# Fused attention, gated MLP and expert attention: values loaded behind the next pair's queries and keys, MLP weights at later ranks, and zeros beside 64-row weights of the experts' tail

## The chip, the cores and the metric

The kernel is one program on one core of a Trainium2 chip. The metric is the device time in microseconds (us), of which less is better. The engines are PE (TensorE, matrix products), DVE (VectorE), ACT (ScalarE), POOL (GpSimd) and SP (SyncE, whose queue issues every load and store here). Each engine takes its instructions in the order in which they stand in its own program, and a wait holds up everything behind it on that engine.

## What is computed

Three stages follow one another: attention with a local or a strided mask, an MLP with a spatial gate, and a mixture of four attention experts of which each token takes two.

```python
B, H, S, D = 4, 8, 576, 64                        # first attention, 8 heads
scores = q @ k.T / 8                              # heads 0-3 local, heads 4-7 strided
mask_local   = (0 <= i - j < 32)
mask_strided = (i - j >= 0) and (i % 32 == j % 32)
x = softmax(where(mask, scores, -1e9)) @ v        # heads side by side: x is 4 x 576 x 512

h = relu(x @ w_in)                                # 512 -> 1024
u, vv = h[..., :512], h[..., 512:]
v_n = (vv - mean(vv)) / sqrt(var(vv) + 1e-6)
x = (u * (w_spatial @ v_n + b_spatial)) @ w_out   # 512 -> 512

logits = x @ w_gate                               # 4 experts, the best 2 weighted by softmax
for e in range(4):                                # causal attention, head dim 64
    a = softmax(causal(x @ wq[e] @ (x @ wk[e]).T / 8))
    out += gate_e * (a @ (x @ wv[e])) @ wo[e]
```

Matrix products in the second and third stage are made of three products each: an operand is split into a high part (`wh`, `xh`, `vh`) and a low part (`wl`, `xl`, `vlo`), and high by high, high by low and low by high are added up.

## The kernel before

The host of the code is a planner, the class `Plan`. Each piece of work is a generator that yields steps of the form (engine or choice of engines, planned cost, what it needs, buffers it takes), and `plan.add(rank, task)` hands it in with a rank. The planner walks through a model of the chip and always takes the step of the lowest rank that can start, so the ranks, the planned costs and the buffers that are free set the order of instructions on every engine and, where a step allows several engines, which one takes it. That order is fixed before the program runs. Buffers are counted: 75 general ones (`c`), 3 for the 512 KB blocks of the MLP's input weights (`w64`) and 8 banks of PSUM. In the first microseconds the planner fills PE's idle time with 128 by 512 products of zeros (`fill`, L217).

First attention. Heads are worked in pairs: of each batch, pairs 0 and 1 are local, 2 and 3 strided. `a1_load` (L443 on) loads a pair's queries `q` and keys `k` (288 KB each) and then its values `v` (576 KB of a local pair, 384 KB of a strided one), all in one task. `a1_scores` makes the scores on PE (L492 local, L502 strided); DVE adds the mask and takes row maxima (L515, L550: nine operations for a local pair, eleven for a strided one, each followed by a small read of the maximum); ACT takes the exponential (L521, L556); DVE sums and inverts (L529, L530); POOL or DVE scales (L532); PE transposes (L577, L579); and `a1_values` multiplies by the values (L635), after which ACT copies the high part `xh` out and DVE makes the low part `xl` (L647).

MLP weights. Of the input weights, four blocks make the half that gives vv (h = 1 in the code) and four the half that gives u (h = 0). `weight` loads a block of 512 KB (L337) and DVE takes it apart with four operations (L344, L345, L346, L349); an addition (L370) and a subtraction (L377), each on DVE or POOL, and a copy of the high part (L310 or L312) make `wh` and `wl`. The v blocks also go through PE (L357 to L359). `v_half` multiplies x by the v blocks (128 by 512 products of L289 to L291), `u_half` the u blocks by x (products of 288 columns, tiles `xh`, `xl` against `wh`, `wl`), and `spatial` the spatial weights (L789 to L791). `u_half` waits for all four u blocks.

Experts' tail. Of a batch's 576 tokens, 512 are worked in four blocks of 128 rows, and the last 64 in a fifth. `a2_tail` takes the last 64 queries of two experts, `a2_tail_turn` transposes their weights into tiles `te` (L1084), and `a2_tail_values` multiplies them by the values (L1144), ten products for a batch and a pair of experts, eight of which contract 128 rows and two 64 rows: batches are paired, and the 64 last tokens of an even batch lie in rows 0 to 63 of a shared tile, those of the odd batch in rows 64 to 127. `values` hands each batch its 64 rows of that tile.

The lines of the main program that order the work of interest:

Of the kernel before, what the change touches and what calls it, by code (L numbers as in the profile page):

```python
# [8 lines left out]
R = dt.float32r  # L9
# [144 lines left out]
def fused(tc, qk, vl, vs, win, wsb, woutT, wp, wo, out):  # L154
# [17 lines left out]
    def C(shape, dtype=F, name="c"):  # L172
        return chunk.tile(shape, dtype, name=nm(name), tag="c")
# [269 lines left out]
    def a1_load(b, hp):  # L443
        local = hp < 2
        order = [(bb, h) for bb in range(B) for h in range(4)]
        n = order.index((b, hp))
        d = 4
        prev = [("a", *order[n - d], 1)] if n >= d else []
        yield "sp", 0.46, [("a1", b)] + prev, dict(c=5 if local else 4)
        qt, kt = C([128, S], F, "q"), C([128, S], F, "k")  # L450
        nc.sync.dma_start(qt, qk[b, hp, :, 0, :])
        plan.dma(128 * S * 4)
        yield "sp", 0.46, (), {}
        nc.sync.dma_start(kt, qk[b, hp, :, 1, :])
        plan.dma(128 * S * 4)
        r = plan.ready
        st = A1[b, hp] = dict(q=qt, k=kt, nk=64 if local else 54, v=[], a={}, x=None)
        plan.set(("qk", b, hp), r - plan.end)
        if local:

            parts = [(128, 512, vl[b, hp, :, 512 * i:512 * i + 512]) for i in range(2)] + [(64, 256, vl[b, hp, :64, 1024:])]
        else:
            parts = [(128, 128 * (j1 - j0), vs[b, hp - 2, :, 128 * j0:128 * j1]) for j0, j1 in ((0, 2), (2, 6))]
        for rows, cols, src in parts:
            yield "sp", 0.46, (), {}
            t = C([rows, cols], F, "v")
            nc.sync.dma_start(t, src)
            plan.dma(rows * cols * 4)
            st["v"].append(t)
        plan.set(("v1", b, hp), plan.ready - plan.end)  # L470

    def a1_blocks(hp, g):
# [369 lines left out]
    def values(b, i):  # L842

        pair, (t0, tn) = b // 2, TB[i]
        yield ("pe", t_mm(260, 3 * STEP['values']), ([("gt", pair)] if i == 4 else [("gs", b, k) for k in range(4)])
               + [("W", ("vg", k)) for k in range(4)], dict(d=1))
        ps = P([128, 260], "d")
        g = [[t[:, k] for t in GT[pair]] if i == 4 else [t[:, t0:t0 + tn] for t in GS[b, k]] for k in range(4)]
        yield from mm3(ps, [(*g[k], *W["vg", k]) for k in range(4)], STEP['values'])
        if i == 4:  # L850
            plan.give("c", 2)
        else:
            proj_done(b)
        st = T.setdefault(b, {})

        yield *out_of(256), (), dict(c=1)
        v = C([128, 512], R, "v")
        hi, lo = (v.rearrange("p (e h d) -> p h e d", h=2, d=64)[:, i] for i in range(2))
        src = ps[:, 0:256].rearrange("p (e d) -> p e d", d=64)
        copy(hi, src)  # L860
        yield "dve", t_dve(256, 2), (), {}
        dve.tensor_sub(lo, src, f(hi))
        if "lg" not in st:
            st["lg"] = sm([128, 5, 4], "lg", 2)
            if b % 2:
                dve.memset(st["lg"][:, 4, :], 0.0)
        dve.tensor_copy(st["lg"][:, i, :], ps[:, 256:260])
        plan.give("d")
        for o in range(1 + (i == 4)):
            T.setdefault(b + o, {})["v", i] = v[64 * o:64 * o + 64] if i == 4 else v  # L870
            plan.set(("vv", b + o, i))

    def gate(b):
# [200 lines left out]
    def a2_tail_turn(b, p, n):  # L1074
        blocks = TAIL_TURNS[n]
        w = 128 * len(blocks)
        yield ("pe", 0.109 * len(blocks), [("ta", b, p)], dict(t=1))
        st = T[b]
        ps = P([128, w], "t")

        r = slice(64 * (b % 2), 64 * (b % 2) + 64) if n == 2 else slice(0, 128)
        for c, i in enumerate(blocks):
            s0 = 512 - r.start if i == 4 else 128 * i
            pe.transpose(ps[:r.stop, 128 * c:128 * c + 128], st["ta", p][:, s0:s0 + r.stop], ident)  # L1084
            plan.count(("tadone", b, p), 5, "c", 1)

        def tiles():
            t = st["te", p, n] = C([128, 2, w], R, "te")[r]
            return t[:, 0], t[:, 1]

        yield from split(ps[r], 1, tiles)
        plan.set(("te", b, p, n))
# [122 lines left out]
    def attention(b, rank):  # L1215
        for hp in range(4):
            plan.add(rank + hp + (0 if b else 0.6 * hp), a1_load(b, hp))
            plan.add(rank + hp, a1_scores(b, hp))
            for g in range(2):
                plan.add(rank + hp, (a1_strided if hp > 1 else a1_local)(b, hp, g))  # L1220
                plan.add(rank + hp, a1_turn(b, hp, g))
            plan.add(rank + hp, a1_values(b, hp))

    attention(0, 0)
    for h in (1, 0):
        for k in range(4):
            plan.add(-0.5 + k if h else 5 + k, weight([("in", h, k)], win, 128 * k, 128, 512 * h, 512, summed=h == 1))
    for s in range(4):
        plan.add(104, weight([("sp", s)], wsb, 128 * s, 128, 0, S, after=[("x",0,3,0)]))
    plan.add(104, spatial_tail())  # L1230
# [118 lines left out]
```

## Time and profile before

| | us |
|---|---|
| median of three runs | 447.96 |
| runs | 448.11, 446.03, 447.96 |
| profiled run, whole | 447.52 |
| profiled run, span of its records | 445.8 |

The profile belongs to one run of 447.52 us, of which 445.8 us is the span and 1.7 us lies outside it. Over the span PE is busy 96% of the time, DVE 72%, ACT 63% and POOL 33%. A row of the profile reads: engine, line of the code, operation, output tile, inputs and shapes; a bracket at its end tells the idle time of that engine ahead of it and what ended that idle time. PEclk is the clock that was granted to PE: 1.00 is 2.4 GHz, 0.50 is 1.2 GHz.

### The profile page before, as it was taken

What the parts mean: (1) busy time and instruction counts of PE and PEld (TensorE: products, weight loads), DVE (VectorE), ACT (ScalarE), POOL (GpSimd) and SP (SyncE); (2) the same over time, 40 slices, a digit from 0 to 9 for tenths busy, and PEclk for the clock granted to TensorE, in tenths of its full rate; (3) what the DMA queues carried; (4) which work ended last, traced back from release to release, by engine and by line L of the source; (5) the groups of instructions that cost most, each with busy time, mean ns of one, the idle gap of its engine ahead of it and who ended that gap; (6) DMA issues with size and microseconds to landing.
All of it is one profiled execution on the core that took longest, in us unless ns stands there. A gap on an engine that the chain in (4) does not pass through costs nothing. (4 is left out here: it accounts for less than half of the span.)

```text
span 445.8 us, 12088 instructions
## 1 busy us (share of the span) xinstructions
PE 426.7 (96%) x4428; PEld 383.8 (86%) x4428; DVE 319.2 (72%) x1151; ACT 282.8 (63%) x920; POOL 148.1 (33%) x240
## 2 busy tenths in 40 slices
PE   7697899999999999999999999999999999999995
PEld 3474589998899889998989999989999999988883
DVE  5779999566712574245999846689789879888863
ACT  4468697557730697221554433896787698789973
POOL 2415798141500263021879910101111111151110
PEclk9889999999999999999999999999999999999999
DMA  8989106500455001400100033721640523351223
GB/s 265 380 290 329 32 4 206 187 1 4 157 177 200 3 4 51 141 1 0 49 1 0 1 84 83 170 56 22 135 107 2 132 57 74 75 151 49 71 96 118
DMA packets 22814, 44.20 MB, mean 99 GB/s; under 512 B 3170, under 2 KB 5218, under 8 KB 22756
## 3 DMA queue, kind: packets, MB, share of 16 engines
q1 hardware_dynamic: 22756, 43.44, 32.7%
q8 instruction: 35, 0.57, 0.5%
q14 instruction: 23, 0.19, 0.1%
HBM read 27.18 MB, written 4.72 MB: 72 GB/s over the span
## 5 line engine op out<-in xcount | busy, mean ns | idle before, releaser
L1005 POOL TENSOR_SCALAR a<-a,asums 128x128 f32<-128x128 f32 (+3 forms) x21 | 17.8, 851 | 107.7 <-DVE asums L1013 27.2
L532 POOL TENSOR_TENSOR a<-a,sums 128x256 f32<-128x256 f32 (+3 forms) x31 | 23.0, 743 | 52.6 <-DVE sums L530 27.8
L972 DVE CUSTOM_DVE_ANT_0 a<-ps,mqk 128x128 f32<-128x128 f32 (+4 forms) x72 | 33.4, 481 | 9.3 <-PE ps L985 7.2
L996 ACT ACTIVATE a<-a,amx 128x128 f32<-128x128 f32 (+1 forms) x64 | 35.6, 558 | 6.5 <-DVE amx L972 5.7
L791 PE MATMUL pd<-wh,vlo 128*128 128x288 f32 x128 | 37.8, 295 | 0.9 <-DVE vlo L694 0.9
L289 PE MATMUL pd<-xh,wh 128*128 128x288 f32 x128 | 38.6, 302 | 0.0
L289 PE MATMUL pd<-gh,fh 128*128 128x288 f32 x128 | 38.3, 299 | 0.1
L789 PE MATMUL pd<-wh,vh 128*128 128x288 f32 x128 | 37.8, 296 | 0.0
L291 PE MATMUL pd<-xh,wl 128*128 128x288 f32 x128 | 37.7, 295 | 0.0
L290 PE MATMUL pd<-xl,wh 128*128 128x288 f32 x128 | 37.7, 294 | 0.0
L291 PE MATMUL pd<-gh,fl 128*128 128x288 f32 x128 | 37.7, 294 | 0.0
L790 PE MATMUL pd<-wl,vh 128*128 128x288 f32 x128 | 37.7, 294 | 0.0
L290 PE MATMUL pd<-gl,fh 128*128 128x288 f32 x128 | 37.7, 294 | 0.0
L521 ACT ACTIVATE a<-a,mx 128x64 f32<-128x64 f32 x72 | 24.0, 337 | 20.0 <-DVE mx L515 20.0
L797 DVE TENSOR_TENSOR u<-pd,u 128x288 f32<-128x288 f32 x32 | 13.9, 453 | 31.7 <-PE pd L794 31.6
L1058 DVE TENSOR_TENSOR e<-pt,e 128x384 fp32r<-128x384 f32 (+1 forms) x48 | 27.5, 597 | 3.8 <-ACT e L310 3.3
L556 ACT ACTIVATE a<-a,mx 128x54 f32<-128x54 f32 (+1 forms) x88 | 28.5, 334 | 0.5 <-DVE mx L550 0.5
L289 PE MATMUL pd<-wh,xh 128*128 128x512 f32 x64 | 26.9, 421 | 0.0
L310 ACT ACTIVATE e<-pt 128x384 fp32r<-128x384 f32 (+1 forms) x48 | 23.7, 522 | 4.7 <-PE pt L1069 3.8
L291 PE MATMUL pd<-wh,xl 128*128 128x512 f32 x64 | 25.2, 394 | 1.5 <-DVE xl L647 1.5
L1003 ACT ACTIVATE a<-a,asums 128x384 f32<-128x384 f32 (+3 forms) x43 | 25.2, 599 | 0.9 <-DVE asums L1013 0.7
L290 PE MATMUL pd<-wl,xh 128*128 128x512 f32 x64 | 25.1, 392 | 0.0
(226 smaller groups left out, 1473.5 us busy)
## 6 DMA issues: line engine op xcount, KB each, us to landing
qk<-qk SPq DMA_DIRECT2D x64, 144.0 KB, 2.6
q<-in_qk_dram SPq DMA_DIRECT2D x16, 288.0 KB, 5.0
k<-in_qk_dram SPq DMA_DIRECT2D x16, 288.0 KB, 5.1
w<-in_win_dram SPq DMA_DIRECT2D x8, 512.0 KB, 6.4
v<-in_vl_dram SPq DMA_DIRECT2D x16, 256.0 KB, 5.5
out_dram<-o SPq DMA_DIRECT2D x16, 256.0 KB, 2.0
v<-in_vs_dram SPq DMA_DIRECT2D x8, 256.0 KB, 5.2
w<-in_woutT_dram SPq DMA_DIRECT2D x4, 512.0 KB, 6.0
```

The costliest lines, as they stand in the source:

```text
L289: pe.matmul(ps, ah, bh, start=i == 0, stop=False)
L290: pe.matmul(ps, ah, bl, start=False, stop=False)
L291: pe.matmul(ps, al, bh, start=False, stop=i == n - 1)
L521: act.activation(a[:, c], a[:, c], AF.Exp, bias=mx[:, c:c + 1], scale=-1.0, accum_out=sums[:, c:c + 1])
L556: act.activation(a[:, j, :w], a[:, j, :w], AF.Exp, bias=mx[:, j:j + 1], scale=-1.0, accum_out=sums[:, j:j + 1])
L789: pe.matmul(ps, vh[:, fs], wh[:, c0:c0 + cn], start=(i == 0), stop=False)
L790: pe.matmul(ps, vh[:, fs], wl[:, c0:c0 + cn], start=False, stop=False)
L791: pe.matmul(ps, vlo[:, fs], wh[:, c0:c0 + cn], start=False, stop=False)
L972: dve.tensor_tensor_reduce(a[:, s0:s0 + sn], ps, mask, op0=ALU.add, op1=ALU.min, scale=-0.125, scalar=m if s0 else 3.0e38, accum_out=m)
L996: act.activation(a, a, AF.Exp, bias=m, scale=-1.0, accum_out=st["sums", e][:, i:i + 1])
L1003: act.activation(a, a, AF.Copy, scale=r)
L1058: dve.tensor_sub(el, ps, f(eh))
```

## The change

There are three edits. First, the loads of a pair's values leave `a1_load` and become a task of their own, `a1_load_v`, which may start once the same pair's queries and keys are issued, and which has a later rank: for batch 0 2.2 above that of the pair's queries and keys, for the other batches 0.5. The buffers are taken apart accordingly, two for queries and keys, three or two for values. Second, the ranks of the four v blocks of the input weights go from -0.5 + k to 0.1 + 1.6 k (k counts the blocks from 0). Third, the fifth block of the experts' tail becomes 128 rows: the values tile is handed on whole, `te` keeps all its 128 rows, and POOL writes zeros into the 64 rows that belong to the other batch of the pair.

```diff
--- before.py
+++ after.py
@@ -446,7 +446,7 @@
         n = order.index((b, hp))
         d = 4
         prev = [("a", *order[n - d], 1)] if n >= d else []
-        yield "sp", 0.46, [("a1", b)] + prev, dict(c=5 if local else 4)
+        yield "sp", 0.46, [("a1", b)] + prev, dict(c=2)
         qt, kt = C([128, S], F, "q"), C([128, S], F, "k")
         nc.sync.dma_start(qt, qk[b, hp, :, 0, :])
         plan.dma(128 * S * 4)
@@ -454,19 +454,23 @@
         nc.sync.dma_start(kt, qk[b, hp, :, 1, :])
         plan.dma(128 * S * 4)
         r = plan.ready
-        st = A1[b, hp] = dict(q=qt, k=kt, nk=64 if local else 54, v=[], a={}, x=None)
+        plan.set(("ld", b, hp))
+        A1[b, hp] = dict(q=qt, k=kt, nk=64 if local else 54, v=[], a={}, x=None)
         plan.set(("qk", b, hp), r - plan.end)
+
+    def a1_load_v(b, hp):
+        local = hp < 2
         if local:
 
             parts = [(128, 512, vl[b, hp, :, 512 * i:512 * i + 512]) for i in range(2)] + [(64, 256, vl[b, hp, :64, 1024:])]
         else:
             parts = [(128, 128 * (j1 - j0), vs[b, hp - 2, :, 128 * j0:128 * j1]) for j0, j1 in ((0, 2), (2, 6))]
-        for rows, cols, src in parts:
-            yield "sp", 0.46, (), {}
+        for i, (rows, cols, src) in enumerate(parts):
+            yield "sp", 0.46, [] if i else [("ld", b, hp)], {} if i else dict(c=len(parts))
             t = C([rows, cols], F, "v")
             nc.sync.dma_start(t, src)
             plan.dma(rows * cols * 4)
-            st["v"].append(t)
+            A1[b, hp]["v"].append(t)
         plan.set(("v1", b, hp), plan.ready - plan.end)
 
     def a1_blocks(hp, g):
@@ -867,7 +871,7 @@
         dve.tensor_copy(st["lg"][:, i, :], ps[:, 256:260])
         plan.give("d")
         for o in range(1 + (i == 4)):
-            T.setdefault(b + o, {})["v", i] = v[64 * o:64 * o + 64] if i == 4 else v
+            T.setdefault(b + o, {})["v", i] = v
             plan.set(("vv", b + o, i))
 
     def gate(b):
@@ -1085,8 +1089,11 @@
             plan.count(("tadone", b, p), 5, "c", 1)
 
         def tiles():
-            t = st["te", p, n] = C([128, 2, w], R, "te")[r]
-            return t[:, 0], t[:, 1]
+            t = st["te", p, n] = C([128, 2, w], R, "te")
+            if n == 2:
+
+                pool.memset(f(t)[64 - r.start:128 - r.start], 0.0)
+            return t[r, 0], t[r, 1]
 
         yield from split(ps[r], 1, tiles)
         plan.set(("te", b, p, n))
@@ -1215,6 +1222,7 @@
     def attention(b, rank):
         for hp in range(4):
             plan.add(rank + hp + (0 if b else 0.6 * hp), a1_load(b, hp))
+            plan.add(rank + hp + (0.5 if b else 0.6 * hp + 2.2), a1_load_v(b, hp))
             plan.add(rank + hp, a1_scores(b, hp))
             for g in range(2):
                 plan.add(rank + hp, (a1_strided if hp > 1 else a1_local)(b, hp, g))
@@ -1224,7 +1232,7 @@
     attention(0, 0)
     for h in (1, 0):
         for k in range(4):
-            plan.add(-0.5 + k if h else 5 + k, weight([("in", h, k)], win, 128 * k, 128, 512 * h, 512, summed=h == 1))
+            plan.add(0.1 + 1.6 * k if h else 5 + k, weight([("in", h, k)], win, 128 * k, 128, 512 * h, 512, summed=h == 1))
     for s in range(4):
         plan.add(104, weight([("sp", s)], wsb, 128 * s, 128, 0, S, after=[("x",0,3,0)]))
     plan.add(104, spatial_tail())
```

What SP issues first, of the kernel before (w is a block of weights, q, k and v are a pair's; the number tells buffers apart):

```order
L337 DMA w_134<-in_win_dram 128x1024
L451 DMA q_136<-in_qk_dram 128x576
L454 DMA k_137<-in_qk_dram 128x576
L467 DMA v_140<-in_vl_dram 128x512
L467 DMA v_142<-in_vl_dram 128x512
L467 DMA v_144<-in_vl_dram 64x256
L337 DMA w_146<-in_win_dram 128x1024
L337 DMA w_148<-in_win_dram 128x1024
L451 DMA q_150<-in_qk_dram 128x576
L454 DMA k_151<-in_qk_dram 128x576
L467 DMA v_159<-in_vl_dram 128x512
L467 DMA v_161<-in_vl_dram 128x512
```

And of the changed kernel:

```order
L451 DMA q_134<-in_qk_dram 128x576
L454 DMA k_135<-in_qk_dram 128x576
L337 DMA w_138<-in_win_dram 128x1024
L451 DMA q_140<-in_qk_dram 128x576
L454 DMA k_141<-in_qk_dram 128x576
L337 DMA w_144<-in_win_dram 128x1024
L471 DMA v_146<-in_vl_dram 128x512
L471 DMA v_148<-in_vl_dram 128x512
L471 DMA v_150<-in_vl_dram 64x256
L451 DMA q_152<-in_qk_dram 128x576
L454 DMA k_153<-in_qk_dram 128x576
L337 DMA w_201<-in_win_dram 128x1024
```

The first block of weights now stands behind the first pair's queries and keys, the second pair's queries and keys stand ahead of the first pair's values, and the third block stands behind the third pair's queries and keys.

What DVE does of the last u block (w_636), of the kernel before:

```order
L647 TENSOR_TENSOR xl_794<-px_711,xh_793 128x12x18
L647 TENSOR_TENSOR xl_794<-px_712,xh_793 128x8x18
L349 SCALAR_TENSOR_TENSOR m_899<-w_562,p_821 128x512
L344 TENSOR_SCALAR a_901<-w_636 128x512
L345 SCALAR_TENSOR_TENSOR a_901<-w_636,a_901 128x512
L346 TENSOR_SCALAR p_902<-a_901 128x512
L529 SCALAR_TENSOR_TENSOR sums_805<-sums_805 128x4
L530 RECIPROCAL sums_805<-sums_805 128x4
L647 TENSOR_TENSOR xl_937<-px_907,xh_936 128x6x18
L647 TENSOR_TENSOR xl_937<-px_908,xh_936 128x6x18
L349 SCALAR_TENSOR_TENSOR m_956<-w_636,p_902 128x512
```

And of the changed kernel, where the last u block is w_748:

```order
L346 TENSOR_SCALAR p_1029<-a_1028 128x512
L349 SCALAR_TENSOR_TENSOR m_1044<-w_652,p_997 128x512
L349 SCALAR_TENSOR_TENSOR m_1055<-w_748,p_1029 128x512
L533 SCALAR_TENSOR_TENSOR sums_912<-sums_912 128x5
L534 RECIPROCAL sums_912<-sums_912 128x5
L370 TENSOR_TENSOR m_1055<-m_1055,a_1028 128x512
L533 SCALAR_TENSOR_TENSOR sums_958<-sums_958 128x4
L534 RECIPROCAL sums_958<-sums_958 128x4
L533 SCALAR_TENSOR_TENSOR sums_1008<-sums_1008 128x5
L534 RECIPROCAL sums_1008<-sums_1008 128x5
L554 ISA a_908,mx_1089<-ps_967,mstr 128x54
...
L377 TENSOR_TENSOR wl_1117<-m_1055,wh_1094 128x512
```

The last two u blocks are now taken apart next to each other. Eight blocks stand ahead of this place in both kernels; in the changed one, a further set of nine row maxima (L519, which was L515) of the second batch does too, as do two more of the operations that make `xl`. The addition (L370) and the subtraction (L377) of the last block are on DVE, with three pairs of sums and eleven row maxima (L554, which was L550, the first of which is shown) between them; before, both stood on POOL. On PE the first product of `u_half` now stands ahead of the 72 small products by values (L639, which was L635) of one pair of the second batch and of seven transposes; before, it stood behind them. The products of zeros (L217) fall from 32 to 28, of which seven (ten before) are ahead of the first scores.

What POOL does in the experts' tail, of the kernel before (it scales the weights `a` by the sums):

```order
L1005 TENSOR_SCALAR a_6368<-a_6368,asums_6345 128x256
L1005 TENSOR_SCALAR a_6387<-a_6387,asums_6345 128x384
L1005 TENSOR_SCALAR a_6474<-a_6474,asums_6456 128x256
L1005 TENSOR_SCALAR a_6549<-a_6549,asums_6548 128x128
L1005 TENSOR_SCALAR a_6599<-a_6599,asums_6548 128x256
```

And of the changed kernel, where L1009 is what L1005 was:

```order
L1009 TENSOR_SCALAR a_6369<-a_6369,asums_6346 128x256
L1009 TENSOR_SCALAR a_6388<-a_6388,asums_6346 128x384
L1095 MEMSET te_6514 64x256
L1009 TENSOR_SCALAR a_6475<-a_6475,asums_6457 128x256
L1009 TENSOR_SCALAR a_6551<-a_6551,asums_6550 128x128
L1009 TENSOR_SCALAR a_6601<-a_6601,asums_6550 128x256
L1095 MEMSET te_6762 64x256
```

Eight such writes of zeros are added, each to 64 partitions by 256 elements, one for each batch and pair of experts. The products by values of the fifth block (L1151, which was L1144) wait for POOL as well as for the copies of `te`. Apart from these, PE's order in the expert stage is the same.

## Rows read from the trace of the kernel before

**Rows 1.** Windows: us; busy us by engine (instructions), PE clock, DMA share, GB/s.

```profile
1.24:61.20 59.96, 49.41 (x899) 33.18 (x900) 48.33 (x232) 39.74 (x187) 29.36 (x64) 0.94 0.70 241
2.96:49.62 46.66, 37.64 (x705) 24.83 (x703) 35.97 (x160) 29.60 (x136) 17.04 (x33) 0.93 0.87 302
19.60:26.40 6.80, 6.54 (x73) 4.42 (x73) 2.88 (x6) 2.41 (x9) 1.09 (x5) 0.50 1.05 375
33.70:51.70 18.00, 12.92 (x280) 8.74 (x276) 17.59 (x69) 12.75 (x57) 11.21 (x14) 1.00 0.67 223
51.70:61.20 9.50, 9.41 (x190) 7.54 (x191) 9.03 (x65) 9.16 (x50) 8.59 (x21) 1.00 0.02 4
61.20:81.20 20.00, 20.00 (x279) 18.90 (x278) 17.90 (x50) 16.31 (x62) 14.82 (x18) 1.00 0.53 170
300.00:440.00 140.00, 138.76 (x960) 127.37 (x959) 116.87 (x413) 110.88 (x297) 24.32 (x41) 1.00 0.31 79
```

**Rows 2.** DVE's waits, 2.9 to 33.8 us: total us, times, longest.

```profile
DVE a L550 <- PE ps L502: 3.1, 2, 2.4
DVE a L344 <- DMA w<-in_win_dram: 2.4, 2, 1.2
DVE xl L647 <- ACT xh L310: 2.0, 1, 2.0
DVE a L515 <- PE ps L492: 1.1, 1, 1.1
DVE sums L529 <- ACT a L521: 1.0, 2, 0.7
```

**Rows 3.** Timeline, first 9 us: start, length (us), instruction.

```profile
1.24 4.45 PE L217 MATMUL pd<-zeros 128*128 128x512 bf16 x10 [1.24 <-DVE zeros L212]
...
4.12 0.43 DVE L344 TENSOR_SCALAR a<-w 128x512 int32<-128x512 int32 x1 [1.16 <-DMA w<-in_win_dram]
...
6.89 1.21 PE L492 MATMUL ps<-k,q 64*32 64x64 f32 x72 [1.20 <-DMA k<-in_qk_dram]
...
7.60 0.22 DVE L515 CUSTOM_DVE_ANT_0 a<-ps,mloc 128x64 f32<-128x64 f32 x1 [1.14 <-PE ps L492]
...
8.90 0.09 DVE L515 DVE_READ_ACCUMULATOR2_ANT mx<- 128x1 f32 x1
```

**Rows 4.** Timeline, last u block and first u product, 48 to 62 us.

```profile
48.30 0.58 DVE L647 TENSOR_TENSOR xl<-px,xh 128x108 fp32r<-128x108 f32 x2
...
48.78 0.84 DVE L349 SCALAR_TENSOR_TENSOR m<-w,p 128x512 f32<-128x512 uint32 x1
...
51.79 0.50 PE L291 MATMUL pd<-wh,xl 128*128 128x512 f32 x1 [1.53 <-DVE xl L647]
...
53.66 0.17 DVE L529 SCALAR_TENSOR_TENSOR sums<-sums 128x4 f32<-128x4 f32 x1 [0.23 <-ACT a L521]
...
53.86 0.18 DVE L530 RECIPROCAL sums<-sums 128x4 f32<-128x4 f32 x1
...
57.38 1.00 DVE L377 TENSOR_TENSOR wl<-st,wh 128x576 fp32r<-128x576 f32 x1
...
61.18 0.29 PE L289 MATMUL pd<-xh,wh 128*128 128x288 f32 x1
```

**Rows 5.** Timeline of PE, experts' tail by values, 419 to 438 us.

```profile
419.94 1.09 PE L1144 MATMUL px<-te,v 128*128 128x128 f32 x8
420.87 0.62 PE L1069 MATMUL pt<-ident,a 128*128 128x128 f32 x4
...
436.69 1.03 PE L1144 MATMUL px<-te,v 128*128 128x128 f32 x6
437.65 0.50 PE L289 MATMUL pd<-wh,ch 128*128 128x512 f32 x1
```

**Rows 6.** POOL: a group (busy us, mean ns), and timeline at 400 us.

```profile
L275 POOL MEMSET alone<- 64x512 f32 x6 | 3.3, 554 | 0.3
...
399.81 2.15 POOL L1005 TENSOR_SCALAR a<-a,asums 128x256 f32<-128x256 f32 x2 [1.87 <-DVE asums L1013]
```

## What was predicted ahead of the run

> **What bounds the kernel now.** I read the busy time by stretches first [rows 1]. From 300 to 440 us PE is busy 138.76 of 140 us: whatever is taken off PE there comes off the time, and hardly anything else does. The front is different. Up to 61.2 us PE is busy 49.41 of 59.96 us, so it stands for 10.5 us. Between 33.7 and 51.7 us it is DVE that never rests (17.59 of 18.00 busy, PE only 12.92), and PE's last wait of the front, 1.53 us at 51.79, ends on DVE's `xl` [rows 4]. From there PE hardly waits (9.41 of 9.50), begins the first product of `u_half` at 61.18, and is full to the first product of `spatial` at 81.2 (20.00 of 20.00).
>
> So DVE sets the pace of the front, and the next thing to read is what DVE waited for ahead of 33.8 us [rows 2]: strided scores 3.1 us, weight blocks 2.4, a copy of `xh` 2.0, local scores 1.1, sums 1.0, together 9.6. From its first wait for data at 2.96 us (4.12 less 1.16 [rows 3]) to the end of its last operation on the last u block (48.78 + 0.84 = 49.62 [rows 4]) DVE works 35.97 of 46.66 us [rows 1], so it is idle for 10.7. The change can shorten the front only by what it takes out of these 10.7 us, less what it adds to the 36.
>
> **First and second edit: the order of loads.** The same bytes are loaded, and no work is removed, so this is a matter of when DVE has something to do. I walk along DVE's new order.
>
> The first pair's queries and keys now come first. They are 576 KB. The 512 KB of the first weights had come in by 4.12 us [rows 3], so they are there at about 4.5. Ten products of zeros took 4.45 us from 1.24 [rows 3]; the seven of now end at about 4.4. Scores at 4.5 and row maxima 0.71 later (7.60 less 6.89 [rows 3]) give 5.2: DVE waits 2.2 us from 2.96. Before it waited 1.16 and 1.14 in these places, so nothing is won here yet, but the maxima are done 2.4 us earlier.
>
> Behind them DVE has the first block of weights, the second pair's nine maxima (1.39 us, from 7.60 to 8.99 [rows 3]) and the second block. With 333 to 375 GB/s (375 is the rate from 19.6 to 26.4 us [rows 1], the lower one an estimate from the 302 of the whole front) the second block, 2176 KB into the queue, lands by 9 us, the third, 3840 KB, by 12.5 to 14, and the fourth, 5888 KB, by 18 to 20; DVE would come to them at about 11, 14 and 20 to 22. The 2.4 us of waits for weights therefore go, except for at most 1 us at the third. The strided scores need their queries and keys (third pair 3328 KB, about 12; fourth 4992 KB, about 17) and PE, on which turns and products by values now stand ahead of the third pair's scores. Of those 3.1 us I leave 1.7, of the 2.0 for `xh` 1.0, of the sums' 1.0 all. With the 2.2 at the start, 0.5 at the weights and the 1.1 that rows 2 do not explain, idle is 7.5 us in place of 10.7. The ends: 4.3 if only the start, the sums and the unexplained remain, and 10.7 if each wait comes back under another name.
>
> Work ahead of the same point: eight weight blocks as before, nine more maxima (1.39) and two more `xl` operations (0.58 for two [rows 4]): 35.97 + 2.0 = 38.0. So the last u block's fourth operation ends at 2.96 + 38.0 + 7.5 = 48.5 us, one microsecond earlier than before, though DVE has then done 2 us of later work as well.
>
> What is late next is the end of this block. It has moved to DVE: an addition and a subtraction of at most 1.00 us each (the row of 576 columns at 57.38 [rows 4]), three pairs of sums at 0.38 (53.66 to 54.04), and eleven maxima at the price of the nine, 0.154 each, 1.7. That is 4.8, so the weights are ready at 53.3. Can PE be there? Its 49.41 busy us lose four products of zeros (0.445 each) and the 72 small products and seven transposes that now stand behind the first u product. The small products are 1.2 by the 72 scores [rows 3], the transposes 1.0 by four in 0.62 [rows 5]: 2.2 in all. 45.4 us of work from 1.24 on end at 46.6, so PE has 6.7 us to spare for waits and the weights decide. The old 61.18, without the 2.2 us that PE now still owes, is worth 59.0. **53.3 against 59.0 is 5.7 us; I take 5.0**, because handovers between PE, ACT and DVE which my walk doesn't have can only be added. The ends are 8.9 (idle 4.3) and 2.5 (idle 10.7). A lower one comes from the clock: from 19.6 to 26.4 us PE was granted 0.50, the 1.2 GHz level, behind a stretch in which it had waited, and was busy 6.54 of 6.80 us [rows 1]. Before, the path there ran over loads and DVE; should such a stretch fall on work that DVE waits for, half of it, 3.3 us, is lost, and the front ends at -1.
>
> The gain must then pass `spatial`, whose first product needs the normalised v from DVE. There DVE was busy 17.90 of 20.00 us [rows 1], so it can follow only if its work has moved too. It is 1.2 us earlier at the last u block and 2.0 us of maxima and `xl` are behind it, against 2.0 for the addition and subtraction. Its list up to the first `spatial` has some operations fewer, since copies went to ACT, which had 3.7 us free there. With the 2.1 idle us this makes about 5, just enough. I count it as passed, with a rival on it.
>
> For the other batches the values come 0.5 of a rank later, but PE's order is unchanged from the late first stage on and DMA is at 0.53 of its time from 61 to 81 us: nothing.
>
> **Third edit: 128 rows in the experts' tail.** The products stay 80 in number. Eight of 128 rows take 0.93 us to the next operation (419.94 to 420.87 [rows 5]), 0.116 each. The last six of the kernel, 436.69 to 437.65, take 0.96; the view folds them into one line, but they are blocks of a kind of which the last two products are the 64-row ones. Six at 0.116 are 0.70, so a pair of 64-row products costs 0.26 more than a pair of 128-row ones. Eight batches and pairs make 2.1 us, in a stretch where PE is 99% busy. I take **2.0**. The end below is 0, if the 0.26 has another cause.
>
> The Trainium skill has rules on both sides of this. "TensorEngine Tiling (Array Packing)", Key Properties, says that changing the tiling mode drains TensorE; by that rule, with which the 0.26 us agrees, the term stays 2.1. "TensorE: Matmul & The Clock Gate", LDWEIGHTS, says that loading the stationary operand goes by its columns and not by its contraction rows; by that alone 64 rows would cost as much as 128, the term would be 0 and the total 442.5.
>
> Eight writes of zeros are added on POOL. One of 64 x 512 took 0.55 us [rows 6], so one of 64 x 256 lies between 0.28 and 0.55. POOL is busy 24.32 of 140 us there [rows 1], so I take 0: its idle time hides them. Without that cover they cost 8 x 0.28 to 8 x 0.55, 2.2 to 4.4. The new wait has PE behind it, and it is the third rival.
>
> **Sum**, against the profiled run of 447.52 us (445.8 in the span, 1.7 outside, which stays; 0.4 below the median of 447.96): 447.5 - 5.0 - 2.0 = **440.5 us**.
>
> **Rivals.** A, the front's gain is partly given back at `spatial`: for it speaks that DVE has 2.1 idle us of 20 there; against it the copies that went to ACT. If only 2 of the 5 pass, 443.5. B, the waits change names and grow: the third and fourth pair's scores stand behind more of PE's work, and DVE idles 13.2 us up to the last u block, 2.5 more than before. Then the front gives 0 and the tail 2: 445.5. For it speaks that PE's order there now mixes turns and products by values into the scores, with the half-rate stretch still to fall somewhere; against it that the loads land in the order of use. C, slower, on POOL: each fifth-block product waits on its zeros behind POOL's scalings. Two scalings took 2.15 us together at 399.81 [rows 6]. If each of the eight waits had one and a half of them ahead, 1.6 us, and the 0.3 us of its own, it would cost 8 x 1.9 = 15 us less the 7 won: 455.5. It decides from an average wait of 0.9 us, where the 7 are eaten. Against it: POOL idles 83% of the time. D, the 64-row products gain nothing: 447.5 - 5.0 = 442.5. E, the walk is too careful and idle falls to 4.3: 447.5 - 8.9 - 2.0 = 436.6.
>
> **Chances.** Forecast (438.5 to 442) 0.41, A 0.18, B 0.14, C 0.06, D 0.09, E 0.12. The range runs from 437 to 447: it leaves out C, about a third of E, and a small part of B, some 0.13 in all. A measurement of this kernel tells about 0.5% (2.2 us) from no change. Faster by more than that: forecast, A, D and E, less a little of A, and a third of B, 0.79. Within it: most of B and a little of A and C, 0.14. Slower: most of C and the front's lower end with the tail at nothing, 0.07.
>
> **What would show it.** In the changed profile: DVE's first row maxima near 5.2 us; no wait of DVE for weights above 1 us; DVE idle of 6 to 9 us up to the last u block; the first product of `u_half` (the first with 288 columns) near 53 to 54 us; the first of `spatial` near 76; from 300 to 440 us of the old scale the same work 2 us shorter, fifth-block products at 0.116 apiece and no wait of PE on POOL. A first u product after 57 us makes the front wrong, a u product on time but `spatial` after 78 makes A right, and waits of PE on `te` from POOL make C right.

## The result: slower by half a percent

The changed kernel takes 449.29 us against 447.14 us for the kernel before (medians of 16 runs each, run side by side), a ratio of 1.0053 with a 95% interval of 1.0039 to 1.0066. The forecast was 440.5 us, with a range of 437 to 447. The profiled run took 450.27 us, 448.5 of them in the span.

Executions of the changed kernel spread over some 5 us (446.6 to 451.4, against 445.8 to 448.3 before). A profile shows one execution, so where a median and a profile differ below, both are given; the one profiled here lies 1.0 us above its median.

Two windows of the profile after, as in [rows 1] (us; busy us by engine and instructions, PE clock, DMA share, GB/s):

```profile
2.96:49.62 46.66, 38.76 (x753) 27.85 (x758) 36.19 (x181) 34.55 (x158) 19.32 (x44) 0.96 0.90 304
...
61.20:81.20 20.00, 15.16 (x198) 13.65 (x192) 16.86 (x31) 14.02 (x49) 11.82 (x12) 0.90 0.60 184
```

From 61.2 to 81.2 us PE was full before (20.00 of 20.00); now it works 15.16. That is where the time went. PE's rows of the timeline there, and some of DVE and ACT (start, length, instruction; the bracket is the idle time ahead and what ended it):

```profile
52.50 0.44 PE L581 MATMUL pt<-ident,a 128*128 128x128 f32 x2 [1.23 <-POOL a L536]
...
53.94 0.40 PE L289 MATMUL pd<-xh,wh 128*128 128x288 f32 x1
...
55.57 0.69 DVE L377 TENSOR_TENSOR wl<-m,wh 128x512 fp32r<-128x512 f32 x1
...
56.31 0.40 PE L291 MATMUL pd<-xh,wl 128*128 128x288 f32 x1 [0.65 <-DVE wl L377]
...
64.11 0.40 PE L289 MATMUL pd<-xh,wh 128*128 128x288 f32 x1 [1.58 <-DVE xl L651]
...
76.74 0.79 ACT L310 ACTIVATE xh<-px 128x216 fp32r<-128x216 f32 x2 [2.04 <-DVE xl L651]
...
77.47 0.82 DVE L651 TENSOR_TENSOR xl<-px,xh 128x216 fp32r<-128x216 f32 x2
...
77.96 0.24 ACT L310 ACTIVATE xt<-xh 128x64 fp32r<-128x64 f32 x1
...
78.25 0.80 PE L289 MATMUL pd<-wh,xt 128*128 128x512 f32 x1 [3.27 <-ACT xt L310]
78.84 0.63 PE L290 MATMUL pd<-wl,xt 128*128 128x512 f32 x1
79.27 0.63 PE L291 MATMUL pd<-wh,xt 128*128 128x512 f32 x1
...
85.35 0.29 PE L793 MATMUL pd<-wh,vh 128*128 128x288 f32 x1
```

The first u product starts at 53.94 us, 7.2 us ahead of the 61.18 before [rows 4] and 0.6 from the 53.3 of the forecast. The first product of `spatial` starts at 85.35, 4.1 us later than its 81.24 before. In between PE waits for DVE twice and then 3.27 us for `xt`: the last 64 rows of each batch of a pair, copied by ACT out of `xh` and DVE's `xl` for the product of `v_tail`. That wait ends in the lower clock (two windows of 4 us, columns as above):

```profile
76.00:80.00 4.00, 1.75 (x4) 1.47 (x5) 2.29 (x6) 3.07 (x14) 0.00 (x0) 0.65 0.92 268
80.00:84.00 4.00, 4.00 (x11) 3.17 (x11) 0.00 (x0) 0.22 (x1) 0.00 (x0) 0.50 0.16 62
```

From 80 to 84 us PE is granted 0.50, the 1.2 GHz level, and the twelve products with xt come 0.43 us apart (78.84 and 79.27) in place of 0.23. The kernel before reached the same product at 78.50 with PE full. So the bill at `spatial` is: the product with xt begins 0.25 us earlier than before; its twelve products take 5.29 us in place of 2.74 (78.50 to 81.24 below), 2.55 more; and twelve u products (1.8 us) that stood ahead of it now stand behind it. 2.55 + 1.8 - 0.25 is 4.1.

How the kernel before stood there (its timeline, ACT's last copies of xt and the PE products that need them):

```profile
77.07 0.25 ACT L310 ACTIVATE xt<-xl 128x64 fp32r<-128x64 f32 x1
...
78.50 0.39 PE L289 MATMUL pd<-wh,xt 128*128 128x512 f32 x1
...
79.31 0.24 ACT L310 ACTIVATE xt<-xh 128x64 fp32r<-128x64 f32 x1
...
79.87 0.26 ACT L310 ACTIVATE xt<-xl 128x64 fp32r<-128x64 f32 x1 [0.32 <-DVE xl L647]
...
80.56 0.39 PE L289 MATMUL pd<-wh,xt 128*128 128x512 f32 x1
...
81.01 0.39 PE L291 MATMUL pd<-wh,xt 128*128 128x512 f32 x1
81.24 0.29 PE L789 MATMUL pd<-wh,vh 128*128 128x288 f32 x1
```

Of each group of three products the third (L291) reads the low part of xt. The last low part was ready at 80.13 us and its product began at 81.01; the high part beside it was ready at 79.55 and its product began at 80.56. There was 0.9 us of slack. The forecast didn't use these rows.

They show one more difference. Of the eight copies that the second batch's rows of xt need, six were done by 77.32 us in the kernel before. In the changed kernel all eight stand on ACT behind the copy of `xh` at 76.74, which waits for DVE's `xl`, and the first of them begins at 77.96.

The tail, in one row each for its 80 products (kernel before, then after; the two times are the first and last start):

```profile
L1144 PE MATMUL px<-te,v x80: 220/275/327, 303.6 to 437.4; 128*128 128x128 f32 x64, 64*128 64x128 f32 x16
```

```profile
L1151 PE MATMUL px<-te,v x80: 218/275/328, 307.9 to 440.3; 128*128 128x128 f32 x80
...
425.05 0.34 PE L1151 MATMUL px<-te,v 128*128 128x128 f32 x2
425.22 0.51 PE L1073 MATMUL pt<-ident,a 128*128 128x128 f32 x3
...
439.70 0.89 PE L1151 MATMUL px<-te,v 128*128 128x128 f32 x6
440.43 0.44 PE L289 MATMUL pd<-wh,ch 128*128 128x512 f32 x1
```

The first product of the tail comes 4.3 us late and the last 2.9 late. Between them 1.4 us are won, 1.5 up to the product behind them (440.43 against 437.65 [rows 5] is 2.8). The front loses 4.3, the tail wins 1.5, and the profile stands 2.8 us behind.

### The profile page after: what moved, and what is told of

Its sections match the earlier page's. It is cut to its first block, busy times and chain, and to the rows that moved or that the text cites. A ratio compares the mean times of both kernels' runs of the same rounds, so it can differ in the third digit from the quotient of the medians.

```text
span 448.5 us, 12076 instructions
## 1 busy us (share of the span) xinstructions
PE 425.0 (95%) x4418; PEld 384.8 (86%) x4424; DVE 316.8 (71%) x1143; ACT 285.9 (64%) x930; POOL 149.1 (33%) x246
## 5 line engine op out<-in xcount | busy, mean ns | idle before, releaser
L1009 POOL TENSOR_SCALAR a<-a,asums 128x128 f32<-128x128 f32 (+3 forms) x21 | 17.7, 850 | 99.5 <-ACT a L1000 25.7
L536 POOL TENSOR_TENSOR a<-a,sums 128x256 f32<-128x256 f32 (+3 forms) x31 | 21.9, 706 | 53.0 <-DVE sums L534 19.6
L291 PE MATMUL pd<-xh,wl 128*128 128x288 f32 x128 | 37.8, 296 | 0.7 <-DVE wl L377 0.7
L291 PE MATMUL pd<-gh,fl 128*128 128x288 f32 x128 | 37.7, 295 | 0.0
L651 DVE TENSOR_TENSOR xl<-px,xh 128x108 fp32r<-128x108 f32 (+4 forms) x48 | 19.2, 432 | 10.4 <-ACT xh L310 10.4
L289 PEld LDWEIGHTS pd<-xh,wh 128*128 128x128 f32 x128 | 24.2, 189 | 2.3 <-DVE xl L651 1.8
L716 POOL TENSOR_TENSOR rstd<-rstd,neghalf 128x1 f32<-128x1 f32 x18 | 11.0, 613 | 44.7 <-DVE rstd L714 13.2
```

Source lines behind the costliest of these rows:

```text
L289: pe.matmul(ps, ah, bh, start=i == 0, stop=False)
L291: pe.matmul(ps, al, bh, start=False, stop=i == n - 1)
```

## The experiments

**Each edit alone.** Four kernels: the tail's edit alone (both places of it, `values` and `a2_tail_turn`), the two edits of the front alone, and each of these two by itself, everything else as in the kernel before. The edits are those of the diff above. (The expectations of the last two count the u products in groups of three; the twelve above are four such groups.)

> The kernel before with the third edit alone (128 rows in the tail's fifth block, zeros by POOL). The trace of the changed kernel runs 4.26 to 4.28 us behind that of before from 127 to 305 us and about 3.0 at 434, so my theory now is that this edit gives about 1.2 us and the front loses 4.3: expected 0.9 to 1.5 us faster than before (ratio 0.9967 to 0.998). The predicted 2.0 would be 0.9955. Rival, that writes of zeros and the wait for POOL eat it: no change or slower.

> The changed kernel with the 64-row tail put back: first and second edit alone, same order of the front as in the changed kernel. Theory (the front loses): 4.0 to 4.5 us slower than before (ratio 1.009 to 1.010), first u product near 54 us and first product of spatial near 85. Rival (the loss is in the tail or a matter of one profiled run): within 1 us of before.

> The kernel before with the first edit alone: values loaded behind, weights at their old ranks. 12 of the u products stand behind the product with xt (four in the changed kernel, none before). If the order of loads of the values makes the loss, it is there: 2 to 5 us slower, PE waiting for xt. If the loss needs the weights' later ranks, within 1 us of before.

> The kernel before with the second edit alone: the four v blocks' ranks from -0.5 + k to 0.1 + 1.6 k. Eight u products stand behind the product with xt. If the later weights make the loss, 2 to 5 us slower, with DVE idle longer ahead of 34 us; if not, within 1 us of before.

| kernel | median us | kernel before | ratio (95%) |
|---|---|---|---|
| tail alone | 444.88 | 446.31 | 0.9964 (0.9944 to 0.9984) |
| front alone | 451.41 | 446.31 | 1.0102 (1.0070 to 1.0133) |
| loads of values alone | 449.92 | 446.31 | 1.0077 (1.0047 to 1.0108) |
| ranks of weights alone | 461.00 | 446.31 | 1.0309 (1.0274 to 1.0344) |

The tail wins 1.6 us (0.7 to 2.5, where 0.9 to 1.5 were expected) and the front costs 4.6 (3.1 to 5.9); together they make the result. The third edit by itself beats both kernels. The rows of the tail's products (tail alone, then front alone) have the same difference as the traces above, 132.5 us from the first to the last against 133.8. All fourteen profiles of this document have it: 132.3 to 132.5 us with 128 rows, 133.8 to 133.9 with 64.

```profile
L1147 PE MATMUL px<-te,v x80: 218/275/327, 301.9 to 434.4; 128*128 128x128 f32 x80
```

```profile
L1148 PE MATMUL px<-te,v x80: 218/276/330, 307.6 to 441.4; 128*128 128x128 f32 x64, 64*128 64x128 f32 x16
```

In the profile of the front alone the first u product comes at 55.39 us and the first of `spatial` at 85.03, where 54 and 85 were expected.

Neither edit of the front is good alone. Of the loads alone, the profiled run was one of the quicker (447.73), its clock stayed up throughout, PE doesn't wait for xt in it, and its tail begins only 0.2 us late (303.8); its other executions reach 452.7. Its executions sort by the mean granted clock: the three at 0.994 or more took 446.1 to 447.7 us, the nine at 0.989 or less 449.3 to 452.7. (Those of the changed kernel don't sort so.) The later weights alone are worst: PE waits 2.26 us up to 54.4 and 3.34 us up to 78.9, the second time for ACT's `vr` and not for xt, and in both waits the clock falls for 6.8 us (from 54.0 and from 77.8); the first u product comes 5.7 us later than before and the first of `spatial` 11.7 later. The loads alone cost 3.4 us, a size that one branch of their expectation had, but with a wait for xt that the profile doesn't show; the ranks alone cost 13.8, where I had 5 as the most. That each costs by itself, and both together hardly more than the loads, neither branch had. Where the longer executions of the loads alone lose their time, and what makes the ranks' 13.8 in full, is open; what follows is about the two together.

**Is it the clock?** Zeros on PE in the wait for xt, on top of the changed kernel:

```diff
     def v_tail(pair):
         ...
         ps = P([128, 512], "d")
+        for _ in range(14 if pair == 0 else 0):
+            pe.matmul(ps, zeros[:, :128], zeros, start=True, stop=True)
```

> The changed kernel with 14 products of zeros (128 x 512, bf16) on PE ahead of the product of `v_tail` with xt, in the same PSUM tile, where PE stands still from 74.7 to 78.25 us; nothing else is moved. Theory: part of the loss is PE's clock, granted 0.50 from 77.2 to 84.0 us behind that wait, in which 12 products of 512 columns took 0.43 us each in place of 0.23. With the zeros the clock stays at 1.00 there: 2.4 to 2.8 us faster than the changed kernel, about as fast as the kernel before. Rival, the clock falls in any case, or the wait alone makes the loss: no change against the changed kernel.

448.19 us, a ratio of 1.0033 (1.0014 to 1.0051) to the kernel before: about 0.9 us better than the changed kernel's 1.0053, where 2.4 to 2.8 were expected, and the intervals overlap. The profile of it shows the part in question:

```profile
79.18 3.19 PE L741 MATMUL pd<-zeros 128*128 128x512 bf16 x13
82.02 0.58 PE L289 MATMUL pd<-wh,xt 128*128 128x512 f32 x1
82.44 0.39 PE L290 MATMUL pd<-wl,xt 128*128 128x512 f32 x1
82.67 0.40 PE L291 MATMUL pd<-wh,xt 128*128 128x512 f32 x1
...
86.58 0.29 PE L795 MATMUL pd<-wh,vh 128*128 128x288 f32 x1
```

With the zeros the products come 0.23 us apart, and from the first product with xt to `spatial` it is 4.56 us in place of 7.10. So the clock's share of 2.5 us is shown where it falls. The zeros cost hardly anything themselves: ACT's first copy of xt for these products ends at 81.90 us, and the first of them begins at 82.02. But the clock doesn't fall there in each execution. In the profile of the front alone, whose front is the same, it stays at 1.00 behind the wait for xt, and from there to `spatial` it is 4.48 us:

```profile
80.55 0.51 PE L289 MATMUL pd<-wh,xt 128*128 128x512 f32 x1 [2.61 <-ACT xt L310]
```

That fits a median that gained only 0.9. The profiled run with the zeros was the longest of the twelve (451.38). Its first u product is 2.8 us later than in the changed kernel's profile, and on the way there PE is granted 0.50 for 6.8 us, from 29.7 to 36.5 us.

**Is it the order on PE?** The product with xt behind the twelve u products, as before:

```diff
-            plan.add(rank + 25, v_tail(b // 2))
+            plan.add(rank + 26, v_tail(b // 2))
```

> The changed kernel with the rank of `v_tail` one higher, so that the 12 u products that stand behind the product with xt stand ahead of it, as in the kernel before. Theory: they fill 1.6 of the 3.3 us of wait, and the first product of `spatial` comes 1.6 us earlier, or 3 to 4 if the shorter wait also spares the clock. Rival, order there has no part in it: no change against the changed kernel.

447.89 us, 1.0030 (1.0007 to 1.0053), a gain of about 1.0 where 1.6 to 4 were expected, again with overlapping intervals. In its profile the wait for xt is 1.04 us (3.27 in the changed kernel), the clock doesn't fall behind it, and `spatial` begins 2.83 us after the first product with xt. Again the profiled run was the longest of its twelve (452.09), with 6.8 us of the lower clock from 30.1 us on.

**Is it DVE's backlog?** From 49.62 to 78.30 us DVE is busy 28.09 of 28.68 us in the changed kernel, and the two subtractions of the spatial weights' tail (L407, L408) stand ahead of the last `xl`. I moved them to POOL, and in another kernel I did that and put the zeros in as well:

```diff
     def spatial_tail():
         ...
-        dve.tensor_sub(wl[96:97, :], mb[96:97, :], f(wl)[96:97, :])
-        dve.tensor_sub(wl[:n, :], m[:n, :], f(hi)[:n, :])
+        pool.tensor_sub(wl[96:97, :], mb[96:97, :], f(wl)[96:97, :])
+        pool.tensor_sub(wl[:n, :], m[:n, :], f(hi)[:n, :])
```

> The changed kernel with the two subtractions of the spatial weights' tail (L407, L408, 1.74 and 1.71 us on DVE from 72.97 to 76.46) moved to POOL, between its operations on vlo; every other row of every engine's order is as in the changed kernel. Theory: DVE, which has no idle time from 49 to 78 us, holds xl and through it xt and PE. Taken off it, xl ends about 3.4 us earlier, PE's wait for xt of 3.3 us falls under 1 us, the clock doesn't fall behind it, and the whole is 3 to 6 us faster than the changed kernel (443 to 446). Rival, PE waits for ACT's own queue or POOL's vlo becomes late: less than 1 us gained, or slower.

> The changed kernel with both: the two subtractions on POOL and the 14 products of zeros (3.0 us) ahead of the product with xt. Theory: if the subtractions on POOL take the wait away, the zeros lie on PE's path and this is up to 3 us slower than the kernel with the subtractions alone; if a wait of 2 us or more is left there, it is equal or faster.

Both gave 1.0055 (1.0024 to 1.0087, and 1.0034 to 1.0077): nothing. In the first the wait for xt is 4.14 us, and the product with xt begins 25.20 us behind the first u product, as with the front alone (25.16) and with the later product (25.20); in the profile of the changed kernel it is 24.31. In the second the zeros waited 2.46 us themselves, for ACT, and then held the product with xt from 78.64, when its first copy was ready, to 81.26, so it tells little of the two together. The timeline of the first (POOL and DVE) tells why, with the changed kernel's rows behind it:

```profile
74.06 1.28 POOL L698 TENSOR_TENSOR vlo<-vr,vh 128x512 fp32r<-128x512 f32 x1
75.41 1.50 POOL L407 TENSOR_TENSOR wl<-mb,wl 1x576 fp32r<-1x576 f32 x1
76.99 1.49 POOL L408 TENSOR_TENSOR wl<-st,wh 64x576 fp32r<-64x576 f32 x1
...
74.08 5.90 DVE L718 TENSOR_SCALAR vr<-vr,mv,rstd 128x512 f32<-128x512 f32 x3
```

```profile
70.52 2.42 DVE L718 TENSOR_SCALAR vr<-vr,mv,rstd 128x512 f32<-128x512 f32 x3
...
72.97 1.74 DVE L407 TENSOR_TENSOR wl<-mb,wl 1x576 fp32r<-1x576 f32 x1
74.75 1.71 DVE L408 TENSOR_TENSOR wl<-st,wh 64x576 fp32r<-64x576 f32 x1
```

Beside POOL's subtractions three normalisations on DVE take 5.90 us in place of 2.42, so the 3.45 us taken off DVE came back. The Trainium skill, "SBUF — State Buffer", Who interferes with whom, says that DVE and GpSimd share a pair of ports: a DVE instruction with two SBUF inputs contends with a GpSimd instruction that reads SBUF, and of one in a two-port mode, which tensor_scalar can enter, and a GpSimd instruction the one that is issued first blocks the other until it ends. The 5.90 us agree with it. By this reading the two subtractions on DVE were lengthened too: they take 0.76 and 0.75 us in the last experiment, where POOL does not subtract beside them, and 1.74 and 1.71 here, beside POOL's `vlo` (72.78 to 75.85). So moving them didn't shorten DVE's way to xt. The work itself was left out next: POOL writes zeros to the low parts (of the spatial weights' last 64 rows, and of the bias), for which it reads nothing. That was done to the changed kernel and, as a control, to the kernel with the tail's edit alone, whose front is that of before:

```diff
-        dve.tensor_sub(wl[96:97, :], mb[96:97, :], f(wl)[96:97, :])
-        dve.tensor_sub(wl[:n, :], m[:n, :], f(hi)[:n, :])
+        pool.memset(f(wl)[96:97, :], 0.0)
+        pool.memset(f(wl)[:n, :], 0.0)
```

> The changed kernel without the two subtractions on DVE (L407, L408, 3.45 us): the low parts of the spatial weights' last 64 rows and of the bias are left out, POOL writes zeros there, which read nothing. All other orders are as in the changed kernel. Theory: DVE has no idle time from 49 to 78 us, and PE's wait for xt is DVE's backlog; with 3.45 us less of it the wait of 3.3 us is gone or under 0.7, and the kernel is 3 us faster than the changed one, 5 to 6 where the clock then doesn't fall (443.5 to 446.5). Rival, the wait is made by ACT's queue or by PSUM and stays: within 1 us of the changed kernel.

> The same part left out of the kernel with the tail's edit alone, whose front is that of the kernel before. There PE is full from 51.8 to 81.2 us and comes to the product with xt at 78.5 without a wait. Theory: DVE's backlog costs nothing there, and this is within 0.7 us of the kernel with the tail alone (about 445). Rival, the subtractions hold the front there as well: 2 us faster or more.

On the changed kernel: 448.23 us, 1.0028 (0.9995 to 1.0061), where 443.5 to 446.5 us were expected; the interval is too wide to tell by itself. Its profile:

```profile
65.00 0.61 PE L289 MATMUL pd<-xh,wh 128*128 128x288 f32 x1 [1.58 <-DVE xl L651]
...
77.75 0.50 PE L289 MATMUL pd<-wh,xt 128*128 128x512 f32 x1 [0.42 <-ACT xt L310]
...
82.20 0.29 PE L793 MATMUL pd<-wh,vh 128*128 128x288 f32 x1
```

The wait for xt is 0.42 us (3.27), the clock stays at 1.00 behind it, and `spatial` begins at 82.20 (85.35). The tail begins at 304.7 (307.9). Counted from the first u product (54.82), xt's product comes at 22.9 us in place of 24.3, so leaving out 3.45 us of DVE's work made xt 1.4 us earlier (2.3 against the 25.2 of the other profiles of this front). The other half of the shorter wait is PE's own lateness: behind the wait of 1.58 us it was granted 0.50 from 64.9 to 68.3 us here, and not in the changed kernel's profile. And this run (447.02) was 1.2 us below its median, the changed kernel's (450.27) 1.0 above. So the profile shows that DVE's backlog holds xt in the changed front; what that costs, these medians don't tell. The control, 0.9973 (0.9950 to 0.9997), is not quicker than the tail alone with its subtractions (0.9964): in the old front the backlog costs nothing.

**The same with nothing left out.** The two subtractions can stand behind the last `xl` by their rank:

```diff
-    plan.add(104, spatial_tail())
+    plan.add(126, spatial_tail())
```

> The changed kernel with the rank of the spatial weights' tail at 126 in place of 104, whole computation kept: the two subtractions (L407, L408) stand on DVE behind the last xl, and on PE four more u products and the first products of v of the second batch stand ahead of the first product of `spatial`. Theory (DVE's backlog ahead of xt is the loss): the wait for xt of 3.3 us falls under 1 us, PE is 3 us or more ahead of the changed kernel by 130 us, 444 to 447. Rival, the wait moves to `spatial`, which needs the same low parts: less than 1 us gained.

> The kernel with the tail's edit alone and the same later rank. Its front has no wait at xt, so by the theory nothing is won: within 0.8 us of the kernel with the tail alone. Rival: a later low part is better in any front, 2 us faster.

On the changed kernel: 445.59 us (444 to 447 expected), 0.9975 (0.9956 to 0.9993), against 1.0053 without: 3.5 us better for a rank, and now faster than the kernel before. PE meets xt without a wait and at the full clock:

```profile
78.19 0.39 PE L289 MATMUL pd<-wh,xt 128*128 128x512 f32 x1
...
85.25 0.29 PE L793 MATMUL pd<-wh,vh 128*128 128x288 f32 x1
```

`spatial` is no earlier than in the changed kernel, 85.25, but twelve v products of the second batch now stand ahead of it (and the same 96 u products as there), and the tail begins at 305.0 (307.9), though this profiled run (447.50) was among the longer ones of its kernel. On the tail's edit alone the same rank gives 444.97, 0.9953 (0.9935 to 0.9971); that is the tail alone (0.9964) within the intervals, as expected. The tail's edit alone and this last kernel are the fastest here, 1.6 to 2.1 us below the kernel before. The front of the change, mended, is worth about nothing.

The later rank moves more than the two subtractions. Of the eight copies of xt for the second batch, six are done by 76.52 us in this kernel, two of them on DVE, where the changed kernel's first begins at 77.96. So the 3.5 us are the price of the wait for xt and of what followed it; how much of the wait is DVE's backlog and how much the place of these copies in ACT's order, no run here separates. A kernel with ACT's order alone changed was not run.

## Why the prediction was wrong, step by step

**The first u product: a number that came right by luck.** 53.94 us against 53.3. But DVE's idle time up to 49.62 us did not fall from 10.7 to 7.5: it is 46.66 - 36.19 = 10.5. The waits changed names, as rival B had it, without growing (changed kernel, DVE's waits from 2.9 to 33.8 us, as [rows 2]):

```profile
DVE a L519 <- PE ps L496: 3.0, 1, 3.0
DVE xl L651 <- ACT xh L310: 2.3, 1, 2.3
DVE sums L533 <- ACT a L560: 1.6, 2, 1.3
DVE a L554 <- PE ps L506: 1.5, 1, 1.5
DVE a L344 <- DMA w<-in_win_dram: 0.6, 1, 0.6
```

The weights' waits went, as walked (0.6 left). The start cost 3.0 in place of 2.2 (first maxima at 5.91), the copies of xh 2.3 in place of 1.0. Against this, the work ahead of the last u block was smaller than the 38.0 us of the sum: that block's last operation ended at 49.45 with 36.0 us done. Two errors nearly cancelled there, 49.45 against 48.5. The next term failed: from there to the last block's `wl` it took 6.8 us in place of 4.8 (55.57 + 0.69 is 56.26), with two of the three sums stretched to 1.25 and 2.35 us (last section), and so the weights were ready at 56.3 and not at 53.3. PE's first u product didn't need them. It came when PE got there, behind its wait for POOL's `a` at 52.50; of its group the twelfth product is the first to read that `wl`, and it waited until 56.31. That `u_half` waits for all four blocks holds for the planner; on the chip the first eleven products (53.94 to 55.36) ran ahead of that `wl`.

**The step that failed: "the gain must then pass `spatial`".** I asked whether DVE would have v normalised by the time PE came, reckoned that it would be about 5 us earlier, "just enough", and took the whole 5.0. Two things were wrong in it. DVE was not 5 us earlier: from 49.62 us on it had work with hardly a pause, and its last `xl` ended at 78.29 us against 79.84, only 1.5 us earlier. It is true that some copies went to ACT, but DVE's operations were also stretched beside POOL (last section), and from the last u block to that `xl` it was busy for 28.2 us, against 29.0 before. And normalised v was not what PE needed first. It was xt, which ACT copies behind a copy of `xh` that waits for DVE's `xl`, with 0.9 us of slack before. So most of PE's lead turned into waits, 0.65, 1.58 and 3.27 us. Leaving 3.45 us of DVE's work out brings xt 1.4 to 2.3 us nearer (the kernel without low parts), and a rank that puts that work later, and with it the copies of xt earlier, wins 3.5 us (the last experiment).

**What I had as rival A was half of it.** The sign that the forecast had named for A came: a u product on time, `spatial` after 78 us. A said that the gain would be partly given back there, 443.5. In fact PE fell behind the old kernel, because this wait cost more than its length: the clock that fell with it took 2.5 us more in the profiled run, and the order, made for a PE that is on time there, had put twelve u products behind the waiting one. I had the lower clock in the working only as the low end of the front's walk (-1), on a stretch near 20 us, and not as a price of waits that the change itself might make.

**The tail: right mechanism, 2.0 in size, 1.5 measured** (1.6 by its own run, 0.7 to 2.5). The 64-row products do cost more than 128-row ones, but 0.26 a pair was too much: it came from one group, compared with a mean of another. The last six take 0.73 us to the next operation in place of 0.96, which is 0.23 less, and two in the middle 0.17 (425.05 to 425.22) in place of 0.36, which is 0.19 less. Over the eight groups with such a pair it is 0.14 to 0.23 each, 1.6 in all, and with that the 1.5 is accounted for. Rival D, that 64 rows cost no more than 128, is refuted (0.9964, 0.9944 to 0.9984, of the tail alone), and with it what the Trainium skill's "TensorE: Matmul & The Clock Gate", LDWEIGHTS, would make of it alone. Rival C is refuted too: PE has no wait on POOL in that stage, and the eight writes of zeros, 0.30 us each, lie in POOL's idle time.

**Still open.** PE's waits in the front that the profile can only name "issue" are larger with the changed order. Between 15 and 34 us, nearly all among the small products by values, they are 2.0, 1.6, 3.4 and 2.0 us in the four profiles with the old front, and 2.8, 4.2, 4.7, 4.3, 4.2, 4.4, 2.4 and 4.6 in the eight with the new one. In seven of these eight, and in one of the four, the clock falls to 0.50 for 3.4 or 6.8 us somewhere between 19 and 37 us; the two in which that is 6.8 us from about 30 us on (zeros, later product) were the longest executions of their kernels. During these waits the 16 DMA engines are busy for a share of 0.93 to 1.08. Whether instructions arrive late there was not tested. This may be part of why gains that a profile shows (zeros, later product, left-out low parts) come out smaller in the medians.

## What to carry to other kernels

Before a lead is counted as won, look for the next places where the engine that gains it meets another one's work, and read the slack there from the trace: when was the last input ready, and when was it taken. Where that is 0.9 us, a lead of 5 becomes a wait, and a wait on PE can cost more than itself through the clock, as the 2.5 us behind the wait for xt did. A small edit that can be had alone (the tail's) should be measured alone, since it was good and was hidden by the rest.

## What the runs showed of the chip that I had not expected

DVE's small operations can last until a POOL operation beside them ends. A sum over 128 x 4 values took 2.35 us, and one over 128 x 5 took 1.25, where a third took 0.14; they end with POOL's subtraction and addition (changed kernel, DVE, then POOL):

```profile
49.38 1.25 DVE L533 SCALAR_TENSOR_TENSOR sums<-sums 128x5 f32<-128x5 f32 x1
51.34 2.35 DVE L533 SCALAR_TENSOR_TENSOR sums<-sums 128x4 f32<-128x4 f32 x1
53.82 0.14 DVE L533 SCALAR_TENSOR_TENSOR sums<-sums 128x5 f32<-128x5 f32 x1
```

```profile
48.94 1.67 POOL L370 TENSOR_TENSOR m<-m,a 128x512 f32<-128x512 f32 x1 [0.57 <-DVE m L349]
...
52.41 1.26 POOL L377 TENSOR_TENSOR wl<-m,wh 128x512 fp32r<-128x512 f32 x1
```

48.94 + 1.67 is 50.61, and the first sum ends at 50.63; 52.41 + 1.26 is 53.67, and the second ends at 53.69. This fits with what moving the two subtractions from DVE to POOL brought, which was nothing.

And the clock. The same wait does not always end in the lower one: the wait of 1.58 us ahead of the u product (64.11 above) stands in all eight profiles of the changed front; in five of them PE was granted 0.50 for 3.4 us from about its end on, and in three, the changed kernel's among them, it kept 1.00. Of the waits for xt, those of 3.27 and 4.14 us were followed by 0.50, and those of 2.61, 1.04 and 0.42 were not.
